# Query features transposed by DMA instead of on TensorE, with the loads planned as one DMA stream, in a linear-attention and feed-forward kernel

One core of a Trainium2 chip. The metric is the device time of one execution in microseconds (us), median of several runs. A run is called slow when it is over 1.5% above the fastest of its kernel in the same session; ratios use the fast runs only.

## The reference

Attention with sketched quadratic features, then a gated feed-forward layer. Cut to what matters:

```python
# q, k, v: (4, 4, 1088, 32); S1, S2: (8, 32); w_gate, w_val: (128, 1536); w_out: (1536, 128)
def phi(x):                                   # 64 features
    a = einsum('rd,bhsd->bhsr', S1, x); b = einsum('rd,bhsd->bhsr', S2, x)
    return einsum('bhsi,bhsj->bhsij', a, b).reshape(*x.shape[:-1], 64)
kv = einsum('bhsf,bhsd->bhfd', phi(k), v);  z = sum(phi(k), axis=2)
attn = (phi(q) @ kv) / (phi(q) . z + 1e-6)
x = attn.transpose(0, 2, 1, 3).reshape(4352, 128)
out = (maximum(x @ w_gate, 0) * (x @ w_val)) @ w_out
```

## The kernel before

The tokens are split into ten *groups* (three of batch 0, two of each later batch, one of remainders). A group needs `kv` of its batch; then its query features `qp` (tokens on partitions) are transposed into `pt` (features on partitions), multiplied by `kv` (`num`), and evacuated into `xT`. The feed-forward part works on `xT` in 102 *units*: gate matmul, relu on ScalarE, value matmul, product `ht` on VectorE, output matmul. The groups start at units 0, 6, 12, 24, 36, 48, 60, 72, 84 and 96.

No engine chooses its order at run time. A planner in the program, `plan()`, sorts all operations by durations written beside them and by `SEM`, the delay it assumes from the end of an operation to its use on another engine. Each engine then works through its fixed list. A gate ties attention work to a unit.

```python
# class Q
def tr(self, x):                     # TensorE: 8 transposes of 128x128 for a group of 4 tiles
    n = self.n
    self.ps = bank(x).bitcast(FP16)[:, 0:2 * n * 128].rearrange("f (k t) -> f k t", t=128)
    for k in range(2 * n):
        nc.tensor.transpose(self.ps[:, k], self.qp[:, 2 * k:2 * k + 2].rearrange("s r f -> s (r f)"), ident)
def tre(self, lo, hi):               # ScalarE: evacuation, twice for a group of 4 tiles
    if lo == 0:
        self.pt = a_kp.tile([128, 2 * self.n, 128], FP16, name="pt")
    nc.scalar.copy(out=self.pt[:, lo:hi], in_=self.ps[:, lo:hi])
# ...
SEM = {"PE": 220.0, "ACT": 220.0, "DVE": 250.0, "POOL": 200.0}
K0, KA, KB, QA, QB = 2, 35, 25, 20, 8
# ... in add_k: half of the first batch's products kp on VectorE
dve = first and hf == 0
phis.append(op("DVE" if dve else "POOL", 640 if dve else 1080, kb.phi, hf, ...))
# ... in add_q
tr = op("PE", 115 * c, qk.tr, deps=tuple(phis), bank=banks, **kw)
tres = [...]                         # op("ACT", 600, qk.tre, ...)
num = op("PE", ..., qk.num, deps=(tre, *kv), bank=banks, **kw)
spread(n0, start[grp] - QA, start[grp] - QB)      # gates of a group's q work
```

## Time and profile before

| | before |
|---|---|
| time | 125.57 us median (124.8 to 126.27), span of the profiled run 123.9 us |
| busy | PE 114.9 us, DVE 97.3, ACT 81.3, POOL 46.8 |
| first feed-forward matmul (gate) | 22.11 us |
| transposes on PE, evacuations on ACT | 68, 17 |

PE is TensorE, DVE VectorE, ACT ScalarE, POOL GpSimd, SP SyncE, which only issues DMA here. A timeline row gives start, duration, engine, line and operation; the bracket at its end is the engine's idle time before it and what ended it. This row of PE's timeline, before, is the end of the start phase:

```profile
22.11 0.38 PE L454 MATMUL bank<-xT,wg 128*128 128x256 f16 x2 [0.48 <-ACT xT L433]
```

### The profile page before, as it was taken

What the parts mean: (1) busy time and instruction counts of PE and PEld (TensorE: products, weight loads), DVE (VectorE), ACT (ScalarE), POOL (GpSimd) and SP (SyncE); (2) the same over time, 40 slices, a digit from 0 to 9 for tenths busy, and PEclk for the clock granted to TensorE, in tenths of its full rate; (3) what the DMA queues carried; (4) which work ended last, traced back from release to release, by engine and by line L of the source; (5) the groups of instructions that cost most, each with busy time, mean ns of one, the idle gap of its engine ahead of it and who ended that gap; (6) DMA issues with size and microseconds to landing.
All of it is one profiled execution on the core that took longest, in us unless ns stands there. A gap on an engine that the chain in (4) does not pass through costs nothing.

```text
span 123.9 us, 2888 instructions
## 1 busy us (share of the span) xinstructions
PE 114.9 (93%) x1117; PEld 80.6 (65%) x1117; DVE 97.3 (78%) x198; ACT 81.3 (66%) x165; POOL 46.8 (38%) x62
## 2 busy tenths in 40 slices
PE   6994899889999999999999999999999999999940
PEld 6864748767877669765665568755655766667920
DVE  3589376587889889397999796788979998979940
ACT  4100004795865649698996578659979988989930
POOL 6959102600593179941510199117005404000000
PEclk9999559999999999999999999999999999999995
DMA  2999990554053507562002100120020011011022
GB/s 49 300 141 192 181 224 6 176 107 158 9 188 55 105 0 177 77 156 100 14 0 41 49 3 0 11 79 0 3 52 33 8 28 57 5 19 65 0 44 83
DMA packets 9521, 9.28 MB, mean 75 GB/s; under 512 B 3364, under 2 KB 7844, under 8 KB 9508
## 3 DMA queue, kind: packets, MB, share of 16 engines
q1 hardware_dynamic: 5228, 6.82, 18.7%
q0 software_dynamic: 4096, 2.25, 14.2%
q8 instruction: 8, 0.13, 0.4%
q10 hardware_dynamic: 184, 0.04, 0.1%
q14 instruction: 5, 0.04, 0.1%
HBM read 9.12 MB, written 2.23 MB: 92 GB/s over the span
## 4 chain that ended last, share of the span: by engine, by line
PE 74%; DVE 11%; DMA 5%; ACT 4%; issue 2%; SPq 1%; ACTq 0%
PE bank L454 16%; PE bank L481 16%; PE bank L466 15%; PE bank L372 8%; DVE ht L471 8%; PE bank L254 5%; DMA q_sb<-in_q_dram 5%; PE bank L409 3%; ACT g_sb L460 2%; PE bank L427 2%; PE bank L302 2%; PE bank L280 2%; PE bank L334 2%; PE bank L155 2%; PE bank L312 1%
## 5 line engine op out<-in xcount | busy, mean ns | idle before, releaser
L471 DVE TENSOR_TENSOR ht<-g_sb,bank 128x512 f16<-128x512 f16 x102 | 65.7, 676 | 11.3 <-ACT g_sb L460 5.3
L460 ACT ACTIVATE g_sb<-bank 128x512 f16<-128x512 f32 x102 | 60.0, 602 | 15.7 <-PE bank L454 13.7
L481 PEld LDWEIGHTS <-ht 128*128 128x128 f16 x408 | 30.3, 98 | 18.4 <-issue 2.0
L481 PE MATMUL bank<-wo,ht 128*128 128x128 f16 x408 | 39.3, 219 | 0.6 <-DVE ht L471 0.6
L454 PE MATMUL bank<-xT,wg 128*128 128x512 f16 (+1 forms) x120 | 38.7, 347 | 0.6 <-ACT xT L433 0.5
L466 PE MATMUL bank<-xT,wv 128*128 128x512 f16 (+1 forms) x120 | 38.3, 347 | 0.4 <-DVE ht L471 0.4
L202 POOL TENSOR_TENSOR qp<-an,abq 128x1024 f16<-128x1024 f32 (+1 forms) x9 | 15.8, 1757 | 8.7 <-DVE an L397 8.1
L202 POOL TENSOR_TENSOR kp<-abk 128x512 f16<-128x512 f32 x14 | 14.5, 1064 | 8.5 <-DVE abk L265 8.5
L384 POOL TENSOR_TENSOR bw<-abq 128x128 f32<-128x128 f32 (+1 forms) x7 | 3.1, 436 | 31.7 <-DVE abq L380 31.7
L466 PEld LDWEIGHTS <-wv 128*128 128x128 f16 x120 | 11.7, 99 | 3.3 <-issue 1.6
L454 PEld LDWEIGHTS <-wg 128*128 128x128 f16 x120 | 11.5, 100 | 3.3 <-issue 2.0
L372 PE MATMUL bank<-qt,wst 128*128 128x512 f32 (+2 forms) x26 | 11.4, 553 | 0.0
L416 ACT COPY pt<-bank 128x512 f16<-128x512 f16 x17 | 10.0, 596 | 1.4 <-PE bank L409 1.4
L254 PE MATMUL bank<-kt,sk 128*128 128x256 f32 x32 | 9.6, 396 | 0.0
L380 DVE STREAM_TRANSPOSE abq<-bank 128x512 f32<-128x512 f32 (+1 forms) x10 | 6.3, 633 | 2.9 <-PE bank L372 2.9
L155 PE MATMUL bank<-zero 128*128 128x128 f16 x88 | 7.5, 256 | 1.1 <-DVE maskw L142 1.1
L155 PEld LDWEIGHTS <-zero 128*128 128x128 f16 x88 | 6.7, 117 | 1.4 <-DVE maskw L142 1.1
L246 DVE STREAM_TRANSPOSE kt<-k_sb 128x512 f32<-128x512 f32 x8 | 5.5, 698 | 1.9 <-DMA k_sb<-in_k_dram 1.9
L324 ACT ACTIVATE kv<-bank 64x64 f16<-64x64 f32 x16 | 3.5, 218 | 5.2 <-PE bank L292 5.0
L433 ACT CAST xT<-bank 128x512 f16<-128x512 f32 (+1 forms) x10 | 5.3, 529 | 2.3 <-PE bank L427 2.2
L280 PEld LDWEIGHTS <-kp 128*128 128x128 f16 x64 | 4.2, 112 | 3.5 <-DVE kp L202 1.9
L280 PE MATMUL bank<-v_sb,kp 128*128 128x64 f16 x64 | 4.8, 206 | 1.8 <-DVE kp L202 1.8
(73 smaller groups left out, 98.7 us busy)
## 6 DMA issues: line engine op xcount, KB each, us to landing
q_sb<-in_q_dram SPq DMA_DIRECT2D x4, 544.0 KB, 7.5
out_dram<-o_sb SPq DMA_DIRECT2D x7, 256.0 KB
k_sb<-in_k_dram SPq DMA_DIRECT2D x3, 512.0 KB, 4.6
v_sb<-in_v_dram POOLq DMA_DIRECT2D x4, 256.0 KB, 5.9
k_sb<-in_k_dram SPq DMA_DIRECT2D x2, 256.0 KB
wg<-in_moe_w_gate_dram POOLq DMA_DIRECT2D x1, 384.0 KB, 7.3
wv<-in_moe_w_val_dram POOLq DMA_DIRECT2D x1, 384.0 KB, 8.6
wo<-in_moe_w_out_dram POOLq DMA_DIRECT2D x1, 384.0 KB, 10.2
```

The costliest lines, as they stand in the source:

```text
L155: nc.tensor.matmul(w_ps[:, 0:128], zero, zero, start=True, stop=True)
L202: eng.tensor_tensor(out=dst.rearrange("s x (i j) -> s x i j", i=R), in0=a_src[:, :, :, None].to_broadcast([dst.shape[0], n, R, R]), in1=ab ...
L254: nc.tensor.matmul(self.ps[h0][:, lo * n * 32:(lo + w) * n * 32].rearrange("p (c x) -> p c x", c=w), sk[:, hf].rearrange("p a b f -> p (a ...
L280: nc.tensor.matmul(self.m[:, p * 64:p * 64 + 64], self.kp[:, hf, c * H + 2 * p:c * H + 2 * p + 2].rearrange("s h f -> s (h f)"), v_sb[self ...
L372: nc.tensor.matmul(self.ps[:, i * w:(i + 1) * w], wst[:, b].rearrange("p h f -> p (h f)"), self.qt.rearrange("p x t -> p (x t)")[:, i * w: ...
L380: nc.vector.transpose(self.absb.rearrange("p x f -> p (x f)"), self.ps[:, 0:n * 128])
L416: nc.scalar.copy(out=self.pt[:, lo:hi], in_=self.ps[:, lo:hi])
L454: nc.tensor.matmul(g_ps[:, y * W:(y + 1) * W], wg[:, j], xT[:, self.col:self.col + W], start=True, stop=True)
L460: nc.scalar.activation(out=self.g_sb, in_=self.g_ps, func=ACTF.Relu)
L466: nc.tensor.matmul(self.v_ps[:, y * W:(y + 1) * W], wv[:, j], xT[:, self.col:self.col + W], start=True, stop=True)
L471: nc.vector.tensor_tensor(out=self.ht, in0=self.g_sb, in1=self.v_ps, op=ALU.mult)
L481: nc.tensor.matmul(o[:, s], self.ht[:, y * W + x * 128:y * W + (x + 1) * 128], wo[:, j], start=(j == 0 and s == 0), stop=(j == NJ - 1), sk ...
```

## The change

The intent: take the query transposes off TensorE, the bound, and their evacuations off ScalarE; let SyncE issue DMA transposes instead. The planner now also sees the loads, as operations of a DMA stream. With it come new distances, another share of work at the start, and another order of the k side. Cut to its core:

```diff
+        def turn(self):
+            self.pt = a_kp.tile([128, 2 * self.n, 128], FP16, name="pt")
+            nc.sync.dma_start(out=self.pt, in_=self.qp.rearrange("s x f -> s (x f)"), transpose=True)
-    SEM = {"PE": 220.0, "ACT": 220.0, "DVE": 250.0, "POOL": 200.0}
+    SEM = {"PE": 220.0, "ACT": 220.0, "DVE": 250.0, "POOL": 200.0, "DMA": 2000.0, "SP": 2000.0}
-    K0, KA, KB, QA, QB = 2, 35, 25, 20, 8
+    K0, KA, KB, QA, QB = 3, 33, 21, 17, 12
+    def load(ns, eng, t, fn, *args, **kw):
+        o = op(eng, t, fn, *args, **kw)
+        return op("DMA", ns, lambda: None, deps=(o,))
     # add_k: first batch's kp all on POOL, half of its kv copies on DVE, z's remainder first
-                dve = first and hf == 0
-                phis.append(op("DVE" if dve else "POOL", 640 if dve else 1080, kb.phi, hf, ...
+                phis.append(op("POOL", 1120 if first else 1080, kb.phi, hf, nc.gpsimd, c, 2, ...
     # add_q
-        tr = op("PE", 115 * c, qk.tr, deps=tuple(phis), bank=banks, **kw)
-        ...
+        if fast:
+            tr = op("PE", 115 * c, qk.tr, deps=tuple(phis), bank=banks, **kw)
+            ...
+        else:
+            tres = [op("SP", 1250, qk.turn, deps=tuple(phis), **kw)]
+            hold("qp", an, tres[0])
+            tre = tres[0]
-                g0 = start[grp] <= 12
+                g0 = start[grp] < 12
     # ... cut: loads wrapped in load(), buffers g 3 and v 3, smaller re-estimates
```

By the words of the change the first three groups stay on TensorE. The last edit makes it two: the group that starts at unit 12 goes by DMA as well, so there are eight DMA transposes.

More of the change, by code (lines that the diff above doesn't have):

```diff
@@ L284, in kv @@
                         v_sb[self.b][:, 2 * p:2 * p + 2, cc * D:(cc + 1) * D],
-                        start=c == 0 and hf == 0 and p == 0, stop=False,
+                        start=c == 0 and hf == 0 and p == 0, stop=c == GC - 1 and hf == 1,
                         skip_group_check=True)
@@ L295, in kv_rest @@
                         vt[rows, 2 * p:2 * p + 2, e * D:(e + 1) * D],
-                        start=False, stop=e == E - 1, skip_group_check=True)
+                        start=False, stop=False, skip_group_check=True)
         def z(self, x, c):
-            if c == 0:
+            if x is not None:
                 self.zps = bank(x)[:, 0:64]
@@ L305, in z, with z_rest @@
                 ab.rearrange("s h (a f) -> s a h f", a=2)[:, :, :, R:2 * R],
-                start=c == 0, stop=False, skip_group_check=True)
-        def z_rest(self, rest):
+                start=x is not None, stop=False, skip_group_check=True)
+        def z_rest(self, x, rest):
+            if x is not None:
+                self.zps = bank(x)[:, 0:64]
             rows = slice(32 * self.b, 32 * self.b + 32)
@@ L313, in z_rest @@
                     self.zps[:, 0:32], ab.rearrange("s h f -> s (h f)"), ab[:, :, R:2 * R],
-                    start=False, stop=e == E - 1, skip_group_check=True)
+                    start=x is not None and e == 0, stop=e == E - 1, skip_group_check=True)
         def zdiag(self):
@@ L320, in zdiag, with kvcopy @@
                 in1=maskz.rearrange("p a h j -> p (a h j)"), op=ALU.mult)
-        def kvcopy(self, g, r):
-            nc.scalar.mul(
-                out=kv16[64 * r:64 * r + 64, self.b, r].rearrange("f (p g) d -> f p g d", g=2)[
-                    :, :, g],
-                in_=self.m[64 * g:64 * g + 64, 0:128].rearrange("f (p g d) -> f p g d", p=2, g=2)[
-                    :, :, g],
-                mul=KVSCALE)
+        def kvcopy(self, g, r, eng):
+            o = kv16[64 * r:64 * r + 64, self.b, r].rearrange("f (p g) d -> f p g d", g=2)[:, :, g]
+            i = self.m[64 * g:64 * g + 64, 0:128].rearrange("f (p g d) -> f p g d", p=2, g=2)[
+                :, :, g]
+            if eng is nc.scalar:
+                eng.mul(out=o, in_=i, mul=KVSCALE)
+            else:
+                eng.tensor_scalar(out=o, in0=i, scalar1=KVSCALE, scalar2=None, op0=ALU.mult)
         def w(self, x):
@@ L411, in tr @@
                     self.qp[:, 2 * k:2 * k + 2].rearrange("s r f -> s (r f)"), ident)
+        def turn(self):
+            self.pt = a_kp.tile([128, 2 * self.n, 128], FP16, name="pt")
+            nc.sync.dma_start(out=self.pt, in_=self.qp.rearrange("s x f -> s (x f)"),
+                              transpose=True)
         def tre(self, lo, hi):
@@ L508, in __init__ @@
             self.holds, self.end = [], None
-    SEM = {"PE": 220.0, "ACT": 220.0, "DVE": 250.0, "POOL": 200.0}
+    SEM = {"PE": 220.0, "ACT": 220.0, "DVE": 250.0, "POOL": 200.0, "DMA": 2000.0, "SP": 2000.0}
     SLACK = (0.0, 60.0, 60.0, 0.0)
-    BUFS = {**dict.fromkeys(range(8), 1), "g": 2, "v": 4, "o": 2, "kt": 3, "qt": 3, "abk": 2, "abq": 2, "kp": 2,
+    BUFS = {**dict.fromkeys(range(8), 1), "g": 3, "v": 3, "o": 2, "kt": 3, "qt": 3, "abk": 2, "abq": 2, "kp": 2,
             "qp": 2, "ktr": 3, "pt": 2, "g_sb": 4, "ht": 8, "bw0": 1, "bw1": 1, "an": 2, "rd": 2, "zd": 2}
@@ L589, with add_rest @@
         units += [F(*grp, i) for i in range(NJ * grp[2] // 4)]
-    T0 = {"PE": 4700.0, "DVE": 2900.0, "ACT": 5300.0, "POOL": 7900.0}
+    T0 = {"DMA": 16500.0, "SP": 4700.0, "PE": 4700.0, "DVE": 2900.0, "ACT": 5300.0, "POOL": 7900.0}
     WGAP, WARM_UNTIL = 250.0, 16000.0
-    K0, KA, KB, QA, QB = 2, 35, 25, 20, 8
-    def add_rest(n, src, at, level, gate):
+    K0, KA, KB, QA, QB = 3, 33, 21, 17, 12
+    def load(ns, eng, t, fn, *args, **kw):
+        o = op(eng, t, fn, *args, **kw)
+        return op("DMA", ns, lambda: None, deps=(o,))
+    def add_rest(n, src, at, level, gate, loaded=()):
         x = Rest(n, src)
         kw = dict(level=level, gate=gate)
-        t1 = op("DVE", 360, x.t1, at=at, **kw)
+        t1 = op("DVE", 360, x.t1, at=at, deps=loaded, **kw)
         ab = op("PE", 240, x.ab, deps=(t1, sk_fill), bank=range(7), **kw)
@@ L604, in add_rest, with add_k @@
         return x, t2, phi
-    def add_k(b, rest, landed, gate, banks, loaded, behind):
+    def add_k(b, rest, landed, gate, banks, k_in, v_in, behind):
         kb = K(b)
@@ L613, in add_k @@
         for pr in range(2):
-            t1s.append(op("DVE", 620, kb.t1, pr, at=landed[pr], deps=tuple(t1s[-1:]), level=lv, **kw))
+            t1s.append(op("DVE", 620, kb.t1, pr, at=landed[pr], deps=(*t1s[-1:], *k_in), level=lv, **kw))
         n = 2 if first else 4
@@ L622, in add_k @@
                                   deps=(*t1s[h0 // 2:(h0 + n) // 2], sk_fill, *abs_[-1:], *behind),
-                                  bank=(None,) if new else banks, level=lv, **kw))
+                                  bank=(None,) if new else banks, level=(3 if h0 == 0 else 2) if first else 0, **kw))
                     abs_.append(new[-1])
@@ L630, in add_k @@
             for hf in range(2):
-                dve = first and hf == 0
-                phis.append(op("DVE" if dve else "POOL", 640 if dve else 1080, kb.phi, hf,
-                               nc.vector if dve else nc.gpsimd, c, 2, deps=tuple(t2s), level=lo_lv, **kw))
+                phis.append(op("POOL", 1120 if first else 1080, kb.phi, hf, nc.gpsimd, c, 2,
+                               deps=tuple(t2s), level=lo_lv, **kw))
         zs = []
+        if first:
+            zs.append(op("PE", 500, kb.z_rest, x, deps=(rest_t2,), level=lv, bank=banks, **kw))
         for c in range(GC):
-            zs.append(op("PE", 330, kb.z, c, deps=(*t2s, *zs[-1:]), level=lv,
+            zs.append(op("PE", 275, kb.z, c, deps=(*t2s, *zs[-1:]), level=lv,
                          bank=(None,) if zs else banks, **kw))
-        zs.append(op("PE", 500, kb.z_rest, x, deps=(zs[-1], rest_t2), level=lv, **kw))
+        if not first:
+            zs.append(op("PE", 500, kb.z_rest, x, deps=(zs[-1], rest_t2), level=lv,
+                         bank=(None,), **kw))
         zd = op("DVE", 200, kb.zdiag, deps=(zs[-1],), level=lv, **kw)
@@ L645, in add_k @@
         for c in range(GC):
-            kvs.append(op("PE", 280, kb.kv, c, bank=(None,) if kvs else banks,
-                          deps=(*phis[c // 2 * 2:c // 2 * 2 + 2], *kvs[-1:], *loaded), level=lo_lv, **kw))
-        kvs.append(op("PE", 300, kb.kv_rest, x, vt, deps=(kvs[-1], rest_phi), level=lo_lv, **kw))
-        hold("abk", t2s[0], kvs[-2])
-        hold("kp", t2s[0], kvs[-2])
+            kvs.append(op("PE", 240, kb.kv, c, bank=(None,) if kvs else banks,
+                          deps=(*phis[c // 2 * 2:c // 2 * 2 + 2], *kvs[-1:], *v_in), level=lv, **kw))
+            if c == 0:
+                kvs.append(op("PE", 300, kb.kv_rest, x, vt, deps=(kvs[-1], rest_phi), level=lo_lv, **kw))
+        hold("abk", t2s[0], kvs[-1])
+        hold("kp", t2s[0], kvs[-1])
         cps = []
@@ L653, in add_k, with add_q @@
             for r in range(2):
-                cps.append(op("ACT", 210, kb.kvcopy, g, r, deps=(kvs[-1], *cps[-1:]), level=lo_lv, **kw))
+                dve = first and g == 1
+                cps.append(op("DVE" if dve else "ACT", 230, kb.kvcopy, g, r,
+                              nc.vector if dve else nc.scalar, deps=(kvs[-1],), level=lv, **kw))
         hold("bank", kvs[0], cps[-1])
+        for c in cps[:-1]:
+            cps[-1].deps += (c,)
         return cps[-1], wf
-    def add_q(grp, n, kv, wf, landed, gate, fast, banks):
+    def add_q(grp, n, kv, wf, landed, gate, fast, banks, q_in):
         qk = Q(*grp, n)
@@ L663, in add_q @@
         rest = grp[0] == B
-        t1 = op("DVE", 560 if rest else 40 + 145 * c, qk.t1, at=landed, **kw)
-        ab = op("PE", 1000 if rest else 60 + 110 * c, qk.ab, deps=(t1, *wf), bank=banks, **kw)
+        t1 = op("DVE", 560 if rest else 40 + 145 * c, qk.t1, at=landed, deps=q_in, **kw)
+        ab = op("PE", 1000 if rest else 60 + 215 * c, qk.ab, deps=(t1, *wf), bank=banks, **kw)
         hold("qt", t1, ab)
@@ L680, in add_q @@
         hold("an", an, phis[-1])
-        tr = op("PE", 115 * c, qk.tr, deps=tuple(phis), bank=banks, **kw)
-        hold("qp", an, tr)
-        tres = []
-        for lo in range(0, 2 * c, 4):
-            tres.append(op("ACT", 600, qk.tre, lo, lo + 4, deps=(tr, *tres[-1:]), **kw))
-        tre = tres[-1]
-        hold("bank", tr, tre)
+        if fast:
+            tr = op("PE", 115 * c, qk.tr, deps=tuple(phis), bank=banks, **kw)
+            hold("qp", an, tr)
+            tres = []
+            for lo in range(0, 2 * c, 4):
+                tres.append(op("ACT", 600, qk.tre, lo, lo + 4, deps=(tr, *tres[-1:]), **kw))
+            tre = tres[-1]
+            hold("bank", tr, tre)
+        else:
+            tres = [op("SP", 1250, qk.turn, deps=tuple(phis), **kw)]
+            hold("qp", an, tres[0])
+            tre = tres[0]
         num = op("PE", 1000 if rest else 50 + 65 * c, qk.num, deps=(tre, *kv), bank=banks, **kw)
@@ L735, in load_rest_q, with load_rest_kv @@
         load_q(nc.sync, b)
-        if b == 1:
-            load_rest(nc.sync, kr, k, range(B))
-            load_rest(nc.sync, vr32, v, range(B))
+    def load_rest_kv():
+        load_rest(nc.sync, kr, k, range(B))
+        load_rest(nc.sync, vr32, v, range(B))
     sketch = Sketch()
@@ L748 @@
     f0 = op("DVE", 420, fill_static, deps=(s_copy,), level=1)
-    rest0 = (*add_rest(32, kr0, 6000.0, 2, -1), vr0)
-    rest = (*add_rest(128, kr, 26000.0, 0, 7), vr)
-    cast = op("ACT", 400, lambda: nc.scalar.copy(out=vr, in_=vr32), gate=9, at=29000.0)
-    kvs, wfs, xs = [], [], []
+    rest0 = (*add_rest(32, kr0, 5500.0, 2, -1), vr0)
+    cast = None
+    kvs, wfs, xs, qs = [], [], [], []
     for b in range(B):
         s = start[b, 0, 2 if b == 0 else GC]
-        lv = ()
+        k_in = v_in = q_in = ()
         if b > 0:
-            lv = (op("POOL", 900, load_main, nc.gpsimd, v_sb[b], v, b, gate=[0, -1, 10, 20][b],
-                     at=13000.0), cast)
-            op("ACT", 200, load_k, b, at=13500.0, gate=[0, -1, 4, 20][b])
-            op("ACT", 200, load_rest_q, b, gate=[0, 0, 10, 24][b])
+            k_in = (load(1650, "ACT", 200, load_k, b, at=13500.0, gate=[0, -1, 4, 20][b]),)
+            q_in = (load(1800, "ACT", 200, load_rest_q, b, gate=[0, 0, 10, 24][b]),)
+            v_in = (load(1650, "POOL", 900, load_main, nc.gpsimd, v_sb[b], v, b,
+                         gate=[0, 0, 10, 20][b], at=13000.0),)
+        if b == 1:
+            kvr = load(600, "SP", 3000, load_rest_kv, gate=0)
+            rest = add_rest(128, kr, 0.0, 0, 7, (kvr,))
+            cast = op("ACT", 400, lambda: nc.scalar.copy(out=vr, in_=vr32), gate=9, deps=(kvr,))
+            rest = (*rest, vr)
+        if b > 0:
+            v_in += (cast,)
+        qs.append(q_in)
         n0 = len(ops)
-        kv, wf = add_k(b, rest if b else rest0, [(4300.0, 5300.0), (19500.0,) * 2, (0.0,) * 2, (0.0,) * 2][b],
-                       s - 40 if b > 1 else -1, range(7), lv,
+        kv, wf = add_k(b, rest if b else rest0, (4400.0, 5600.0) if b == 0 else (0.0, 0.0),
+                       s - 40 if b > 1 else -1, range(7), k_in, v_in,
                        (first_ab,) if b == 1 else ())
@@ L774 @@
                               2 if start[grp] == 0 else 1 if g0 else 0,
-                              range(7))
+                              range(7), q_in)
                 xs.append(x)
@@ L782 @@
     x, _ = add_q(groups[-1], len(xs), tuple(kvs), tuple(wfs), 0.0, start[groups[-1]] - 20, 0,
-                 range(7))
+                 range(7), sum(qs, ()))
     xs.append(x)
```

## The prediction

> **What bounds the kernel now.** I read the page first (its slices, then its chain), then the rows of the groups, then the timeline of PE and of VectorE at the start and at the end. The slices:
>
> ```profile
> PE   6994899889999999999999999999999999999940
> POOL 6959102600593179941510199117005404000000
> PEclk9999559999999999999999999999999999999995
> ```
>
> A slice is 3.1 us. From slice 8 (some 25 us) to slice 37 PE never falls below 90%. Before that stands a start of 22 us in which little of the feed-forward part runs, and in two of its slices PE has half its clock. The chain and the rows that matter:
>
> ```profile
> PE 74%; DVE 11%; DMA 5%; ACT 4%; issue 2%; SPq 1%; ACTq 0%
> ...
> L471 DVE TENSOR_TENSOR ht<-g_sb,bank 128x512 f16<-128x512 f16 x102 | 65.7, 676 | 11.3 <-ACT g_sb L460 5.3
> ...
> L202 POOL TENSOR_TENSOR qp<-an,abq 128x1024 f16<-128x1024 f32 (+1 forms) x9 | 15.8, 1757 | 8.7 <-DVE an L397 8.1
> ...
> L416 ACT COPY pt<-bank 128x512 f16<-128x512 f16 x17 | 10.0, 596 | 1.4 <-PE bank L409 1.4
> ```
>
> Three quarters of the chain are PE. A busy PE could still be an idle one whose matmuls are drawn long (379 ns for 512 columns), so I take the distance from start to start instead. At the end of the PE timeline it is 0.22 us for 512 columns and 0.22 us for four of 128, that is 56 ns each; in the chain in order of time eight transposes take 0.45 us, the same 56 ns; an fp32 product of 256 columns takes 0.46 us, one of 512 takes 0.87. With such distances, all matmuls after the first gate matmul (at 22.1 us) come to 94.1 us: 67 for the feed-forward part, 27 for the attention. The last matmul ends at 119.7 us, so this part takes 97.6 us and PE is really at work for 96% of it. PE's throughput bounds it; ScalarE and VectorE do not, though VectorE is near: 83.2 us busy from 22 to 120 us. In the last 10 us a unit costs PE three times 0.22 us and VectorE 0.64 to 0.68 us: a tie.
>
> The start is another thing, a chain of latencies:
>
> ```profile
> 9.92 3.17 DVE L202 TENSOR_TENSOR kp<-abk 128x512 f16<-128x512 f32 x2
> 13.01 0.21 DVE L318 TENSOR_TENSOR zd<-bank,maskz 128x64 f32<-128x64 f32 x1
> 14.38 0.19 DVE L339 TENSOR_TENSOR wst<-bank,maskw 128x32 f32<-128x32 f32 x1 [1.16 <-PE bank L334]
> 15.88 0.45 DVE L380 STREAM_TRANSPOSE abq<-bank 128x256 f32<-128x256 f32 x1 [1.31 <-PE bank L372]
> ...
> 17.38 0.69 DVE L202 TENSOR_TENSOR qp<-an,abq 128x512 f16<-128x512 f32 x1
> ```
>
> Two products kp on VectorE take 3.17 us, and zd, which the q side needs, stands behind them until 13.01 us. It could have run from about 10.6 us on.
>
> **What the Trainium skill says.** "VectorE: DVE Perf Modes", The three transpose paths: a 128x128 transpose of 2-byte data takes 390 ns on TensorE and 1309 ns through the DMA crossbar. The trace agrees on a TensorE latency of that size (L409 is drawn at about 390 ns for a group of four), but pipelined it costs PE only 56 ns; no run yet shows the crossbar. "DMA: Bandwidth & Descriptors", Latency and other measured facts: a DMA transpose was measured at 261 GB/s; and Anatomy of one DMA gives a fixed cost of some 2.0 us (for the GpSimd path). One group's pt is 128x1024 fp16, 256 KB, so my estimate from that page is 1.0 + 2.0 us, and with the sequencer some 3.3 us from issue to landing. The same page, Queues, rings and completion order: an engine takes a ring's descriptors in order. So a transpose on SyncE stands behind the loads that SyncE issued before it; a k load of 512 KB took 4.6 us to land here. "Advanced Engine Details and Errata", GPSIMD Details: GpSimd shares ports with VectorE and conflicts with its instructions of two SBUF inputs. The trace agrees: the 128x512 product took 1.6 us on VectorE beside GpSimd products, and 0.69 us (qp above) with GpSimd idle.
>
> **The change part by part.** The order of instructions shows that the text of the change is off by one: the third group (start at unit 12) also goes by DMA. There are 8 DMA transposes, seven of 128x8x128 and one of 128x4x128; 8 of the 68 PE transposes stay.
>
> 1. *PE.* 60 transposes leave, all from after the first gate: 60 x 56 ns = 3.36 us. Nothing else on PE changes in number but 14 warming matmuls at the start. Work after the first gate is 94.1 - 3.3 = 90.8 us; at the same 96%, 94.2 us in place of 97.6: 3.4 us less.
> 2. *ScalarE.* 15 of 17 evacuations leave: 15 x 596 ns = 8.9 us of 81.3. ScalarE is off the path; worth nothing by itself.
> 3. *VectorE.* Two kp products (3.2 us) go to GpSimd, two kv copies (some 0.45 us) come. All before the first gate, so VectorE's load in the long part stays at 83 us, below PE's 91.
> 4. *The start.* In the new order zd follows the q transposes directly. I step through with the old durations: abk ends at 9.1 us (held by the q load, which lands at 7.97), the two q transposes end at 10.1, zd at 10.6, the w product at 11.5, wst at 11.8, first q product 12.6, abq 13.3, then bw, dn, rd, an and qp as before 2 us more: 15.2 us in place of 18.07. On the other side GpSimd now does kpr and four kp in a row from 8.95 us: five times 1.04 us ends at 14.2, the kv products at 14.8, the copies, shared by two engines, at about 16.2. So PE transpose 15.5, evacuation to 16.5, num at 17.0, xT at 17.5: first gate at about 17.8 us, or later if the clock falls to half as before. I put 18.2 in place of 22.1: 3.9 us less. This, not the transposes, is the larger half.
> 5. *What it adds.* On the latency of a group: before, tr, evacuation twice and the semaphores took some 2.2 us; now 0.2 + 3.3 us. Where a group's num stands close behind its qp in PE's fixed order, PE waits. Two places look tight. Third group: GpSimd's qp ends near 23.9 us by the same stepping, its transpose lands at 27.4, and PE comes to its num after 8.4 us of work, at 27.0: 0.5 us. First group of batch 1 (gate 24): from the q product to the end of qp the trace before shows 4.75 us (41.75 to 46.49); plus 3.5 us is 8.3, and the new order gives PE 7.4 us of work between: 0.7 us. The groups after have about 10 us or more of work between. With loads in the ring before them I give 1.7 us in all.
>
> Sum: 125.57 - 3.9 - 3.4 + 1.7 = 120.0 us.
>
> **The rivals.** *First: the transpose is slow, and its wait takes the place of the one removed.* If one takes 6 us or more, alone or behind a k or q load, each group waits some 2 to 3 us at least in the two tight places and about 1 us in some of the other six: 5 to 9 us, and 123 to 127 us in all. For it: no trace shows one, and SyncE is one in-order queue with loads and stores, each with its own wait on ScalarE; before, its stores wait for ScalarE for up to 13 us. Against it: DMA is busy only 0 to 2 tenths after slice 22, and the order lets most groups have their features many units early. *Second: VectorE becomes the bound.* PE's saving comes in stretches where attention is dense; in the others the two tie at 0.65 us a unit, and PE's saving turns into waits for ht. For it: the tail's tie, and VectorE at 7.7 of 8 us from 94 to 102 us. Against: from 46 to 54 us VectorE has 5.7 of 8. This would halve the 3.4: 121.7 us. *Third: the start gains little*, as PE falls to half its clock again and GpSimd's four kp set the pace; first gate at 20.5 us, 122.3 us in all. Before, two slices at half clock follow a gap of 1.76 us on PE; the new order has warming matmuls in its gaps, which speaks against. *Fourth, to the good side*: no tight place waits, 118.3 us, and a first gate at 17 us makes 117.
>
> **Range and chances.** The terms' errors are about 1.2 us for the start, 1 for PE's share, and 2 to the bad side for the transposes. I take 117.0 to 123.5 us. Faster by over 2% means below 123.06 us; it needs about 2.5 of the 7.3 us of gains to survive, and only a slow transpose with a failed start undoes it: 0.87. Within 2% 0.09, slower 0.04.
>
> **What would show each step.** Right: first gate matmul at 17 to 19 us; zd at about 10.5 us; PE idle near 27 us and ahead of the num at gate 24, each at most 1.5 us; transposes landing in 3 to 4.5 us; VectorE's busy time lower by about 2.5 us and ScalarE's by about 9; last matmul near 114 us. Wrong: waits of PE for pt from the DMA of more than 3 us in sum (first rival), more idle of PE for ht in the middle at a prompt pt (second), half clock from 12 to 18 us and a first gate past 20 us (third).

## The result

| | before | changed |
|---|---|---|
| median, runs side by side | 125.92 us (4 runs, 124.8 to 127.82) | 129.74 us (129.28 to 129.88, and a slow run of 135.12) |
| ratio | 1 | 1.032, 95% interval 1.022 to 1.043: slower |
| first gate matmul | 22.11 us | 17.33 us |
| last output matmul starts | 119.3 us | 122.5 us |
| busy | PE 114.9, DVE 97.3, ACT 81.3, POOL 46.8 | PE 111.3, DVE 95.2, ACT 74.3, POOL 49.7 |

A ratio is the mean time of one kernel's fast runs over the mean of the other's of the same rounds, so it isn't quite the ratio of the medians. The output is correct.

The page of the changed kernel: PE and its clock in 40 slices (3.2 us each), the engines of the chain that ended last, and the row of `num`:

```profile
PE   6999689935999999699999769993999999999940
PEclk9999999995599999769999999999999999999995
PE 50%; DMA 18%; DVE 11%; POOL 11%; issue 4%; ACT 2%; DVEq 1%; SPq 0%; POOLq 0%
L437 PE MATMUL bank<-pt,kv 128*32 128x256 f16 (+2 forms) x104 | 4.0, 249 | 7.6 <-DMA pt<-qp 7.6
```

Against the lines of before: the solid row of 9s has holes; PE's part of the chain fell from 74% to 50%, and DMA transposes took 18%. PE stood 7.6 us ahead of `num`, all of it waiting for `pt`. Who waited for whom (total, times, longest), first PE's longest wait of before from 24 us to 104 us, then that of the changed kernel:

```profile
PE bank L466 <- DVE ht L471: 0.4, 1, 0.4
```

```profile
PE bank L437 <- DMA pt<-qp: 7.6, 4, 3.5
```

The start went as planned. The changed kernel's timeline:

```profile
9.56 4.13 POOL L202 TENSOR_TENSOR kp<-abk 128x512 f16<-128x512 f32 x4
...
10.34 0.23 DVE L321 TENSOR_TENSOR zd<-bank,maskz 128x64 f32<-128x64 f32 x1 [0.58 <-PE bank L303]
...
14.57 0.69 DVE L202 TENSOR_TENSOR qp<-an,abq 128x512 f16<-128x512 f32 x1
...
17.33 0.38 PE L464 MATMUL bank<-xT,wg 128*128 128x256 f16 x2 [0.48 <-ACT xT L443]
```

`zd` runs at 10.34 in place of 13.01 us, and the feed-forward part begins 4.8 us earlier. So the changed kernel needs 127.5 - 17.3 = 110.2 us from there to its end, before 123.9 - 22.1 = 101.8 us: 8.4 us more for the same feed-forward work and 3.4 us less of transposes. The chain in order of time shows where (start, length; the pieces of DMA alone):

```profile
22.86 7.13 DMA pt<-qp
...
47.96 3.65 DMA pt<-qp
...
67.81 6.51 DMA pt<-qp
...
82.99 5.44 DMA pt<-qp
```

Each is the time from a transpose's issue to its landing, the moment at which the engine that waits is told that the data are there. What happens around the first, in windows (stretch, length; busy time of PE, PEld, DVE, ACT, POOL; clock; DMA share; GB/s):

```profile
27.00:30.00 3.00, 0.00 (x0) 0.00 (x0) 0.73 (x2) 0.00 (x0) 2.75 (x3) 0.80 1.26 215
30.00:33.00 3.00, 2.97 (x20) 2.00 (x21) 1.56 (x3) 0.58 (x1) 1.78 (x3) 0.50 0.36 138
33.00:36.00 3.00, 3.00 (x18) 2.31 (x18) 0.95 (x2) 0.60 (x1) 0.68 (x1) 0.56 0.00 0
```

PE does nothing for 3 us, and then works at half clock for nearly 6 us more. The Trainium skill, "TensorE: Matmul & The Clock Gate", Part 1: The HAM clock gate, says that about 3.4 us without activity gate the clock to half, and that it needs a busy window of that size to come back. This trace agrees in kind: a gap of 3.51 us, then 0.50 and 0.56. It doesn't agree on the threshold. The mean of 0.80 from 27 to 30 us is 0.6 us of lost clock, so 1.2 us at half: the clock fell at about 28.8 us, only 2.3 us into the gap that began at 26.5. At 52.7 us it fell after gaps of 0.39 and 0.68 us, and after those of 1.76 and 1.99 us (at 74.37 and 88.56 us) it stayed at 1.00. What decides isn't shown here.

### The profile page after: what moved, and what is told of

It reads as the page before. It is cut to its first block, busy times and chain, and to the rows that moved or that the text cites. A ratio compares the mean times of both kernels' runs of the same rounds, so it can differ in the third digit from the quotient of the medians.

```text
span 127.5 us, 2813 instructions
## 1 busy us (share of the span) xinstructions
PE 111.3 (87%) x1043; PEld 76.8 (60%) x1043; DVE 95.2 (75%) x196; ACT 74.3 (58%) x148; POOL 49.7 (39%) x66
## 3 DMA queue, kind: packets, MB, share of 16 engines
HBM read 9.12 MB, written 2.23 MB: 89 GB/s over the span
## 4 chain that ended last, share of the span: by engine, by line
PE 50%; DMA 18%; DVE 11%; POOL 11%; issue 4%; ACT 2%; DVEq 1%; SPq 0%; POOLq 0%
DMA pt<-qp 18%; PE bank L476 11%; PE bank L491 10%; PE bank L464 10%; DVE ht L481 6%; POOL qp L202 5%; PE bank L155 4%; PE bank L376 3%; POOL kp L202 3%; PE bank L437 2%; PE bank L254 2%; PE bank L303 2%; DVE abq L384 1%; PE bank L338 1%; POOL v_sb L87 1%
## 5 line engine op out<-in xcount | busy, mean ns | idle before, releaser
L470 ACT ACTIVATE g_sb<-bank 128x512 f16<-128x512 f32 x102 | 59.2, 598 | 21.9 <-PE bank L464 17.7
L491 PEld LDWEIGHTS <-ht 128*128 128x128 f16 x408 | 31.2, 100 | 18.5 <-issue 1.4
L476 PE MATMUL bank<-xT,wv 128*128 128x512 f16 (+1 forms) x120 | 40.0, 358 | 0.1
L202 POOL TENSOR_TENSOR kp<-abk 128x512 f16<-128x512 f32 x16 | 16.5, 1061 | 6.4 <-DVE abk L265 6.4
L464 PEld LDWEIGHTS <-wg 128*128 128x128 f16 x120 | 12.3, 103 | 3.0 <-issue 1.5
L437 PE MATMUL bank<-pt,kv 128*32 128x256 f16 (+2 forms) x104 | 4.0, 249 | 7.6 <-DMA pt<-qp 7.6
L376 PE MATMUL bank<-qt,wst 128*128 128x512 f32 (+2 forms) x26 | 9.6, 471 | 0.0
L437 PEld LDWEIGHTS <-kv 128*32 128x32 f16 x104 | 1.5, 95 | 11.5 <-DMA pt<-qp 7.0
L499 ACT ACTIVATE o_sb<-bank 128x512 f32<-128x512 f32 (+1 forms) x10 | 5.3, 532 | 3.8 <-PE bank L491 3.8
L401 POOL TENSOR_TENSOR an<-abq,rd 128x128 f32<-128x128 f32 (+1 forms) x8 | 3.1, 390 | 9.2 <-DVE rd L396 9.2
```

The lines of the kernel that those rows point to most:

```text
L202: eng.tensor_tensor(out=dst.rearrange("s x (i j) -> s x i j", i=R), in0=a_src[:, :, :, None].to_broadcast([dst.shape[0], n, R, R]), in1=ab ...
L376: nc.tensor.matmul(self.ps[:, i * w:(i + 1) * w], wst[:, b].rearrange("p h f -> p (h f)"), self.qt.rearrange("p x t -> p (x t)")[:, i * w: ...
L437: nc.tensor.matmul(o[32 * h:32 * h + 32, i * w:(i + 1) * w], kv16[:, b, r, h], self.pt[:, i * w:(i + 1) * w, 32 * h:32 * h + 32], start=Tr ...
L464: nc.tensor.matmul(g_ps[:, y * W:(y + 1) * W], wg[:, j], xT[:, self.col:self.col + W], start=True, stop=True)
L470: nc.scalar.activation(out=self.g_sb, in_=self.g_ps, func=ACTF.Relu)
L476: nc.tensor.matmul(self.v_ps[:, y * W:(y + 1) * W], wv[:, j], xT[:, self.col:self.col + W], start=True, stop=True)
```

## The experiments

The question after the result: is it the plan, the traffic of the transposes, or their lateness; and why are they late, when the one at 93.1 us landed in 2.8 us?

First four. Before on that chip: 125.32 us median of 7.

**e1, no DMA transposes, new plan.**

```diff
-        if fast:
+        if True:
```

> The changed kernel with every group's features turned on PE again (no DMA transpose at all); the new plan stays. Theory A (the transposes land late, because they stand in SyncE's one ring behind loads and stores, and PE's fixed order waits for them and then runs at half clock) and theory B (a DMA transpose is slow by itself or slows its neighbours): the waits for pt go, the early first gate (17.3 us) stays, PE does 3.3 us more: about 121 us. Theory C (the new plan's order is the loss, whoever turns the features): 126 us or more.

Measured: 120.43 us (119.97 to 120.81), ratio 0.963 (0.956 to 0.971). First gate at 17.54 us, no wait for `pt`, clock 0.995. The plan alone gains 4.9 us, all of it in the start: from the first gate to the end e1 takes 119.1 - 17.5 = 101.6 us, as long as before. The DMA transposes, with the order that the planner makes around them, cost the changed kernel 9.2 us. Theory C falls.

**e2, the third group on TensorE too.**

```diff
-        if fast:
+        if fast or start.get(grp) == 12:
```

> The changed kernel with the third group too turned on PE, as the words of the change say. Theory A: the wait of 3.5 us near 30 us and the half clock after it go, at the price of 0.45 us of PE; the later waits (0.4, 1.8, 2.0 us) stay: 124 to 126 us. Theory B: the same here. Theory C: 129 us, and the gap near 30 us stays for another cause.

Measured: 135.32 to 135.60 us in the fast runs, and 143.12 for the profiled one, whose start was slow (see e11). A miss for every theory: the wait near 30 us went, yet the time grew by 6 us. The planner had shuffled everything after it, and the other transposes met worse places: PE waited four times for `pt`, 12.1 us in all. **e12** is the same text once more, for a profile without the slow start:

> e2 once more, the same text, for a profile with the first gate at 17.5 us, which e2's profiled run lacked. Theory A2: transposes issued within 1 us of a store's issue land after 6 to 6.5 us; PE waits some 10 us for pt in all, more than the changed kernel's 7.6, because the new order leaves less work ahead of each num; 135 us.

Measured: 142.64 us, with the slow start again (first gate at 23.36 us), so that aim was missed; but the same four waits, 11.8 us in all, stand in it. Of its stores and transposes on SyncE's queue two pairs are typical: store issued at 70.41, transpose at 71.17, `num` released at 77.52 us; store at 86.58, `num` at 93.66 us.

**e3, the loads and stores off SyncE's ring.**

```diff
-        load_main(nc.sync, k_sb[b], k, b)
+        load_main(nc.scalar, k_sb[b], k, b)
     # likewise load_q of the later batches, and the stores of the main groups
```

> The changed kernel with the later k and q loads and the big stores issued from ScalarE, so that after the start SyncE's ring carries the transposes and the small kr and vr loads only. Theory A: each transpose lands in 2.8 to 4 us (in place of up to 7.1), PE's waits for pt fall from 7.6 to below 2 us: 121 to 124 us. Theory B (transposes slow by themselves, or by sharing the 16 DMA engines whatever the ring): landing times stay at 5 to 7 us beside a load or store, and the time at 128 us or more. ScalarE pays some 16 issues of 0.4 to 0.6 us.

Measured: 129.14 and 130.82 us in the fast runs (134.3 and 145.2 in slow ones). Theory A in its first form falls: the order within one ring is not the cause. PE still waited 8.0 us, and a transpose on SyncE's ring was late beside a store on ScalarE's. From its two rows, the issue of the store (ScalarE's queue) and PE's `num` after it; the transpose was issued at 68.11 us and landed after 6.6 us:

```profile
67.97 0.55 ACTq L502 DMA_DIRECT2D out_dram<-o_sb  x1
```

```profile
74.80 0.40 PE L437 MATMUL bank<-pt,kv 128*32 128x256 f16 x8 [0.49 <-DMA pt<-qp]
```

The skill's "DMA: Bandwidth & Descriptors", Queues, rings and completion order, says two things that matter here: an engine takes turns between the rings that have work, and the write that reports a DMA's completion lands only after every earlier write of that engine, across its queues. In the prediction I had leaned on ring order alone. The second rule would let a store on any ring delay the report of a transpose. The 6.6 us here don't need it: the packets (at the end of the experiments) show that the data themselves came late.

**e4, DMA transposes alone, in the plan of before.**

```diff
+        if start.get(grp) not in (0, 6, 12):
+            tres = [op("SP", 1250, qk.turn, deps=tuple(phis), **kw)]     # and turn(), SEM["SP"] = 2000
```

> The kernel before with only the DMA transposes in place of PE's for the groups after the third (SyncE 1.25 us and 2.0 us to landing in its plan). Theory A: PE has 2.9 us less work, but some transposes stand behind a store and come 2 to 4 us late: 124 to 128 us. Theory B: 127 us or more, with every transpose late. Theory C (plan, not transposes): 122.5 us.

Measured: 127.37 us (126.86 to 127.54), ratio 1.018 (1.011 to 1.026), by the 2% rule unclear, by the interval slower. 2.9 us less work for PE turned into 2 us more. One wait of 2.0 us stands out, ahead of the first group of batch 1, whose transpose (issued at 46.08 us, right after a k load at 45.38) landed after 5.7 us; a stretch at half clock follows (mean 0.51 from 52.7 to 56.2 us). In the profiles, e4 takes 124.8 - 21.6 = 103.2 us from the first gate to the end, where 101.8 - 2.9 = 98.9 would be before's time without these transposes. Of the 4.3 us between, the wait and the lost clock (3.5 x 0.49 = 1.7 us) make some 3.7 by this estimate.

So a second form of theory A: **A2, a transpose alone lands in under 3 us, but one issued beside another large transfer, on whatever ring, lands when that one is done; the plan allows 3.25 us.** Next four; before on that chip 125.72 us.

**e5, stores cut to 16 KB**.

```diff
-                        "(k s) t m -> k t s m", s=n),
-                    in_=o_sb[:, 0:n])
+                        "(k s) t m -> k t s m", s=n)[0, :, 0:1],
+                    in_=o_sb[0:32, 0:1])
```

> The changed kernel with its stores of the main groups cut to 16 KB each (wrong result on purpose; same instructions in the same order). Theory A2 (a transpose lands late when another large transfer is in flight, on whatever ring, since alone it lands in 2.4 to 2.8 us): the two transposes issued at 67.8 and 83.0 us, which landed after 6.5 and 5.4 us with a 256 KB store in flight, land in under 3.5 us; PE's waits for pt fall from 7.6 to about 4 us; the wait near 30 us, beside loads, stays: 125 to 127 us. Rival (lateness has nothing to do with the stores): no change in landing, 129.5 us.

Measured: 123.16 and 124.69 us in fast runs (two slow ones at 126.89 and 128.4), 5.0 to 6.6 us less than the changed kernel and less than either theory said. The view of the tile `pt` and PE's waits:

```profile
DMA to landing us min/median/max: 2.4/2.8/3.5
```

```profile
PE bank L437 <- DMA pt<-qp: 4.9, 2, 4.6
```

The order of instructions is the same, only the stores are small: the two late transposes beside stores are now in time (the landing line covers those whose landing the trace shows). The first one, beside loads, still costs 4.6 us. This shows that stores made the later ones late. The clock from 52 to 58 us, 0.62 and 0.81 in the changed kernel (below), is 1.00 here.

**e6, the traffic without the wait**: e1, plus the same eight DMA transposes into a tile that nobody reads.

```diff
+            if self.col >= 4 * 128:
+                unread = a_kp.tile([128, 2 * n, 128], FP16, name="unread")
+                nc.sync.dma_start(out=unread, in_=self.qp.rearrange("s x f -> s (x f)"), transpose=True)
```

> The variant with all features turned on PE (e1, 120.4 us) plus the same eight DMA transposes of the same tiles, issued at the same places, into a tile that nobody reads; every engine but SyncE keeps its order. Theory A2 (what costs is PE waiting for a late pt, not the traffic): 120 to 121.5 us, same as e1. Theory B (the transposes' traffic itself slows loads, stores or the engines): 123 us or more.

Measured: 120.29 and 120.67 us in its fast runs (two slow ones at 126.6 and 126.8), e1's time. The traffic costs nothing. Theory B falls; what costs is the waiting.

**e7, only where there is time, and with time allowed.**

```diff
-        if fast:
+        if fast or start.get(grp) <= 36:
-    ... "SP": 2000.0}
+    ... "SP": 4500.0}
-    K0, KA, KB, QA, QB = 3, 33, 21, 17, 12
+    K0, KA, KB, QA, QB = 3, 33, 21, 22, 14
```

> The changed kernel with the groups up to the one that starts at unit 36 turned on PE, only the later five (48, 60, 72, 84, 96) by DMA, the plan told 4.5 us to landing after the issue in place of 2.0, and the q work of a group begun earlier (22 to 14 units ahead in place of 17 to 12). Theory A2: a pt planned for 5.75 us after its features is in time nearly always, PE's waits for pt below 1 us, and 36 transposes (2.0 us of PE) less than e1: 117.5 to 119.5 us. Theory B: no better than e1 with the same gates, 121 us or more.

Measured: 118.18 and 118.49 us in fast runs (two slow ones at 124.6 and 125.0). No wait of PE for `pt` at all. In these fast runs it is faster than both kernels.

**e8, the control for e7's distances**: e1 with `QA, QB = 22, 14`.

> e1 (all turned on PE) with the q work begun 22 to 14 units ahead in place of 17 to 12: the control for e7's gates. Both theories: within 1 us of e1, 119.5 to 121 us; if it is as fast as e7, the gates and not the transposes gained there.

Measured: 126.09 to 126.50 us, all four. A miss: all four had the slow start (first gate at 23.44 us in its profile), so it decided nothing. But it gave the slow start away. PE's first rows, e8 and then e7 in a fast run:

```profile
1.06 3.81 PE L155 MATMUL bank<-zero 128*128 128x128 f16 x34 [1.06 <-DVE maskw L142]
...
6.25 2.02 PE L254 MATMUL bank<-kt,sk 128*128 128x256 f32 x4
```

```profile
1.06 3.50 PE L155 MATMUL bank<-zero 128*128 128x128 f16 x34 [1.06 <-DVE maskw L142]
...
5.65 1.13 PE L254 MATMUL bank<-kt,sk 128*128 128x256 f32 x4 [0.17 <-DVE sk L181]
```

The same four fp32 matmuls take 2.02 us in e8 and 1.13 in e7: PE works at half its clock. (The first row alone doesn't tell: e1 and the changed kernel also have 3.81 us there, and their fp32 matmuls run at full clock.) It goes on until about 20 us, and the first gate comes at 23.44 us instead of 16.91, 6.5 us later. The clock row of the page doesn't show it; this is e8's:

```profile
PEclk9999999999999999999999999999999999999996
```

So the *slow start*: the 34 warming matmuls at the head of the program (on zeros, read by nobody) sometimes fail to bring PE to full clock. The profiles of e2, e6, e8 and e12 show it directly, all in plans with the new start. Where a slow run of such a kernel wasn't profiled (the changed kernel's 135.12 us, for one, 5.5 us over its others), I infer it from the 6 us. From the first gate to the end e8 takes 124.8 - 23.4 = 101.4 us and e7 116.5 - 16.9 = 99.6, so these distances by themselves gain nothing over e1 (101.6), and the five DMA transposes of e7 gain 1.8 us, by one profile of each.

Four more. Before on that chip: 125.33 us median of 11.

**e9, the changed kernel with the later loads moved away from the first transpose.**

```diff
-            k_in = (load(..., load_k, b, at=13500.0, gate=[0, -1, 4, 20][b]),)
+            k_in = (load(..., load_k, b, at=13500.0, gate=[0, -1, 13, 20][b]),)
     # likewise the q loads (10 to 13) and the v loads (10 to 13) of batch 2
```

> The changed kernel with the loads of batch 2 (k, q, v) begun at unit 13 in place of units 4 and 10, so that the first DMA transpose (issued near 22.9 us) goes out before them. Theory A2: it lands in some 3 to 4 us in place of 7.1, PE's wait of 3.5 us near 30 us and the half clock after it shrink to under 1 us; the later waits beside stores remain (4 us, with some shift): 123 to 126 us. Rival (the first transpose is late for another cause): the wait near 30 us stays over 3 us, 129 us.

Measured: 131.26 to 131.78 us in fast runs (one slow, 139.29). The mechanism came as expected, the time didn't. PE's two rows of `num` after the first transpose (issued at 22.61 us) and after its worst one:

```profile
27.19 0.40 PE L437 MATMUL bank<-pt,kv 128*32 128x256 f16 x8 [0.47 <-DMA pt<-qp]
...
107.02 0.40 PE L437 MATMUL bank<-pt,kv 128*32 128x256 f16 x8 [3.42 <-DMA pt<-qp]
```

The wait that was 3.51 us is 0.47: loads had made the first transpose late. But the plan moved again: three waits beside stores are 2.23, 2.41 and 3.42 us, and one of 1.74 us follows a transpose issued 3.4 us after a q load.

**e10, e7's choice of groups without its time**: `"SP": 2000.0` and `QA, QB = 17, 12` again, all else as e7.

> e7 (only the five late groups by DMA, 118.2 and 118.5 us in its fast runs) with the plan's 2.0 us to landing and the changed kernel's own distances (17 to 12 units). Theory A2: the late groups' transposes beside a 256 KB store land after 5 to 6.5 us again, planned for 3.25: PE waits 2 to 5 us in all for pt, 120 to 123 us in fast runs. Rival (the choice of groups alone made e7 fast, not the time allowed): 118.3 us and no waits.

Measured: 128.30 us in one run, 131.2, 132.63 and 138.34 in the others; the first gate of the profiled one (132.63) stands at 17.46 us, so the start wasn't slow. Every run is longer than the 120 to 123 us that theory A2 said, and why the four differ so much isn't shown. PE's waits for `pt`, in the profiled run:

```profile
PE bank L437 <- DMA pt<-qp: 9.1, 3, 4.6
```

With the same five transposes, e7 waits for none. So the choice of groups didn't make e7 fast, but the times at which its plan issues and uses the transposes (4.5 us allowed in place of 2, gates 14 to 22 units ahead in place of 12 to 17). Two things changed there at once, which these runs don't part: `num` comes later after its transpose, and no 256 KB transpose stands close behind a store any more (the nearest follows 4.9 us after one; the last, half as large, follows after 2.2 us and lands after 4.1; here three follow after 0.6 to 1.0 us, and one took 7.7 us to land).

**e11, e7 with a longer warm-up.**

```diff
-    WARM0 = 34
+    WARM0 = 56
```

> e7 with 56 warming matmuls at the start in place of 34. Theory W (the slow runs of the new plan, 6 us longer, are those in which the 3.8 us of warming matmuls did not bring PE to full clock, so that PE ran at half clock from 5 to 20 us): with some 1.2 to 2 us more of them all runs start at full clock, no run near 124.8 us, fast runs 0.5 to 1 us longer than e7's: 118.5 to 119.5 us. Rival (the slow runs come from elsewhere): slow runs in some of the six still.

Measured: 119.14 to 120.24 us in all six runs, ratio 0.971 (0.961 to 0.982; by the 2% rule unclear, as one run of before was 122.6 us and only it and those near it counted as fast). No slow start, no wait for `pt`; the first gate is at 18.93 us, 2 us later than in e7. That is more than was said: the median of 120.18 us is 1.8 us over e7's fast runs, not 0.5 to 1.

Two things were open after these twelve: what the transposes are worth when nothing waits (e8 hadn't told by time), and whether a shorter warm-up holds. Two last ones; before on that chip 125.58 us median of 7.

**e13, e8 with 56 warming matmuls**, the control of e11.

> e8 (all features turned on PE, q work begun 22 to 14 units ahead) with 56 warming matmuls, so that the start is the same as e11's. Theory A2 with the prediction's term for PE (a transpose costs PE 56 ns, 36 of them 2.0 us): 2 us longer than e11, 121.5 to 122.5 us. Rival (the gain of e7 over e1 is the gates): 120.2 us, as e11.

Measured: 120.51 to 122.05 us, median 121.37, ratio 0.967 (0.960 to 0.975), no slow start. From the first gate to the end it takes 120.2 - 19.0 = 101.2 us, e11 118.5 - 18.9 = 99.6. So by one profile each, both pairs (e8 and e7, e13 and e11) say 1.6 to 1.8 us for 36 transposes moved off TensorE and waited for by nobody. The profiled run of e13 is its longest; by the medians of all runs e13 takes 1.2 us more than e11, just under what theory A2 said. So the worth is 1.2 to 1.8 us; counted at 56 ns each, 2.0.

**e14, e7 with 44 warming matmuls.**

> e7 with 44 warming matmuls, between its 34 (half of the runs start at half clock) and e11's 56 (none of six). Theory W: fewer slow starts than with 34, perhaps still one of four; fast runs 118.4 to 119.5 us, between e7's and e11's.

Measured: 118.69 to 120.20 us, median 118.86, ratio 0.951 (0.942 to 0.960). First gate at 17.46 us, no slow start, no wait for `pt`. The view of the tile `pt`, five transposes, none of 256 KB close behind a store:

```profile
DMA to landing us min/median/max: 2.8/3.4/4.1
```

This is the best version here: the new start, transposes by DMA for the five late groups, issued early enough. With 34 warming matmuls (e6, e7, e8) 8 of 12 runs were some 6 us longer; with 44 or 56 (e11, e13, e14) none of 14 was. That is a count, not a proof that 44 always suffice, and the twelve ran on another chip than the fourteen. On the chip of the fourteen, with 34, e12's one run had the slow start and one of e9's four was 7.6 us longer; on a third chip e1 had none in four. And e13's profile shows a late rise of the clock:

```profile
1.06 6.08 PE L155 MATMUL bank<-zero 128*128 128x128 f16 x56 [1.06 <-DVE maskw L142]
...
7.89 1.08 PE L254 MATMUL bank<-kt,sk 128*128 128x256 f32 x4
```

All 56 took 109 ns each, half rate (e8's 34 took 112; at full clock it is 56 ns), and the fp32 matmuls after them run at full clock. In e11 (5.96 us for 56) it came little earlier. By my estimate a warm-up of 44 would have ended at about 5.9 us (1.06 + 44 x 0.109), before that rise.

**What a neighbour does to a transpose**, from the rows of all these runs (256 KB each, as the stores are):

| case | us from the transpose's issue to landing or to `num` |
|---|---|
| nothing beside it: changed at 93.1 us, e4 | 2.8, 2.7 |
| small stores (e5) | 2.4 to 3.5 |
| store issued 0.75 and 1.7 us before, same ring: changed | 6.5, 5.4 |
| store issued 0.1 us before, another ring: e3 | 6.6 |
| store issued 2.2 us before, 128 KB transpose: e7, e14 | 4.1, 4.1 |
| beside loads: changed (first), e4, e3 | 7.1, 5.7, 8.9 |

With a store ahead, `num` is released 7.0 to 7.3 us after the *store's* issue: changed 67.06 to 74.37 and 81.27 to 88.56, e9 61.63 to 68.87 and 77.93 to 85.24, e10 61.84 to 68.86 and 76.26 to 83.60, e12 70.41 to 77.52 and 86.58 to 93.66. (In e10 and e12 one more each took 8.5 and 8.6 us.) So the transpose lands when the store is done. It isn't a lack of bandwidth, as the windows of the changed kernel around the transpose of 67.81 us show (columns as above):

```profile
68.00:71.00 3.00, 3.00 (x24) 2.04 (x22) 3.00 (x6) 2.04 (x5) 0.00 (x0) 1.00 0.24 40
71.00:74.00 3.00, 1.61 (x6) 0.52 (x4) 2.05 (x4) 0.85 (x2) 0.45 (x1) 1.00 0.91 135
```

For 3 us the DMA engines are a quarter busy at 40 GB/s, 0.12 MB; most of the two transfers' 0.52 MB moves only after that. Is it the data that are late, or only the report that they have landed? The packets tell: the transpose's are under 512 B, the store's 2 KB. From the view `--dma` of the changed kernel, 67.0 to 70.4, 70.4 to 72.9 and 72.9 to 75.0 us:

```profile
DMA packets 29, 0.06 MB, mean 17 GB/s; under 512 B 0, under 2 KB 0, under 8 KB 29
...
DMA packets 563, 0.32 MB, mean 128 GB/s; under 512 B 464, under 2 KB 464, under 8 KB 563
...
DMA packets 596, 0.14 MB, mean 69 GB/s; under 512 B 596, under 2 KB 596, under 8 KB 596
```

For 2.6 us after its issue no packet of the transpose moves, and more than half move after the store's last. The one at 93.13 us, alone, moved from 94.3 to 95.4. e3, with the store on another ring, shows the same: no small packet before 70.6 us, 621 after 73.3. So beside a store the data are late, not only the report. The store is slow by itself: before, with no transpose near, the one issued at 64.22 us moved until 69.5. In e4, beside loads, it is otherwise: 1040 small packets moved from 48.6 to 50.1 us, 48 after, and `num` was released only at 51.87; there the report was late, which the skill's rule on completions (under e3) would allow. Why a store holds up a transpose's data, on whatever ring, stays open.

## Why the prediction was wrong

- **Step 4, the start: right.** First gate 17.33 us where 18.2 was said, 4.8 us gained where 3.9 was; `zd` at 10.34 where 10.5 was said. e1 shows it alone: 4.9 us faster.
- **Step 1, TensorE: right in count, too large.** 1.2 to 1.8 us of the counted 2.0 for 36 transposes; scaled to 60, 2.0 to 3.0 us in place of 3.4 (an estimate).
- **Steps 2 and 3: right that neither engine is on the path.** ScalarE 7.0 us less busy where 8.9 was said, VectorE 2.1 where 2.5 was.
- **Step 5, what the change adds: this failed.** It said "I give 1.7 us in all". The third group's transpose was to land at 27.4 us and landed at 30.0, after 7.1 us: a wait of 3.51 us in place of 0.5. The rest of that line was near (issue at 22.86 us, PE ready at 26.5 where 27.0 was said); the 3.3 us to landing failed. Gate 24 was right (0.39 and 0.68 us where 0.7 was said). "The groups after have about 10 us or more of work between" was plainly wrong: PE reached the `num` of the transposes issued at 67.8 and 83.0 us so early that it waited 1.76 and 1.99 us. The duration of a lone transpose was estimated well (2.8 us for 3.0 to 3.3); I put it in for transposes that have a store or load beside them, where it is 5.4 to 7.1.
- **A term not in the sum at all: the clock after a wait.** PE works on at 0.50 and 0.56 after the first wait and, at the stretch of gate 24, where it also has gaps, at 0.62 and 0.81:

```profile
52.00:55.00 3.00, 2.32 (x15) 1.43 (x11) 1.31 (x4) 1.86 (x4) 2.22 (x4) 0.62 0.45 97
55.00:58.00 3.00, 3.00 (x30) 1.87 (x30) 1.98 (x4) 1.59 (x3) 0.57 (x1) 0.81 0.96 160
```

Lost in these four windows of 3 us: 3 x (0.50 + 0.44 + 0.38 + 0.19) = 4.5 us. My estimate of the balance: 7.6 us of waits + 4.5 of clock - 2.0 to 3.0 of transposes saved = 9.1 to 10.1 us; the changed kernel minus e1 is 129.6 - 120.4 = 9.2 us, though in two sessions. So close a fit is partly luck: in the stretch at 52 us PE was busy for only 2.32 of 3 us, so not all of the clock lost there was wanted.

- **The rivals.** The first had the mechanism (a slow transpose behind other transfers, its wait in place of the work removed) and said 5 to 9 us of waits (measured 7.6) and 123 to 127 us; without the clock the time was still too short, and its ring order isn't the cause (e3). I gave it too little weight, because the DMA engines were nearly idle; idle engines said nothing about latency. The second, VectorE as the bound, isn't seen: e14 gains by the transposes. The third, a failing start, is wrong for the fast runs and right for those with a slow start, by another cause than the one I gave: the 34 warming matmuls don't always suffice.
- **Two readings in the prediction were off, without weight for the sum.** PE's row shows an 8 in slice 8, so its 90% hold from slice 9 (28 us) on. And the 390 ns of L409 are the span of four transposes; one is drawn at 219 ns, so the trace does not agree with the page's 390 for one.
- **Open:** why a store holds up a transpose's data; what sets the clock after a short gap; and which of e7's two changes (the later `num`, or the distance to the stores) does the work.

## What to carry to other kernels

A DMA's duration by itself isn't its latency beside other transfers: allow, in a fixed plan, for the load or store that will be in flight, or issue it where nothing waits soon. Work taken off the bound is worth its time only as long as nothing waits for its replacement; a stall of TensorE can cost clock as well (3 x (0.50 + 0.44) = 2.8 us after the one of 3.51 us, nothing seen after those of 1.76 and 1.99). Look at the rows of the first matmuls after the warm-up, not only at the clock row, to see whether it has worked.

## What the Trainium skill lacked or had wrong

- "DMA: Bandwidth & Descriptors" gives a rate for a DMA transpose but no latency beside other transfers. A 256 KB transpose alone took 2.4 to 2.8 us, a little under the 3.0 us estimated from the page's rate and fixed cost; behind a 256 KB store 5.4 to 6.6 us, beside loads 5.7 to 8.9 us. The page does say that DMAs from several engines run on the same DMA engines and interleave; e3 (6.6 us on a ring of its own) agrees.
- No page gives the time of a single store to HBM: before, one of 256 KB, issued at 64.22 us, moved until 69.5; a 256 KB transpose issued 0.75 us after a 256 KB store landed 3.7 us later than alone, while for 3 us the DMA share was 0.24.
- "TensorE: Matmul & The Clock Gate" says that about 3.4 us of activity bring full clock, that the count varies from run to run, and for a benchmark it advises a warm-up of at least 4 us. Here 3.4 to 3.8 us of warming matmuls (34) weren't enough in 8 of 12 runs, and half clock then lasted to about 20 us; 4.4 us (44) were enough in 4 of 4, but in e13 full clock came only after some 6 us. The page's gap of about 3.4 us isn't what decides here: the clock fell 2.3 us into a gap, and at 52.7 us after gaps of 0.39 and 0.68.
- The same page warns that clock events in a trace are not to be fully trusted. e8 is a case: its clock row shows full clock while fp32 matmuls take twice their time (2.02 for 1.13 us).
- "VectorE: DVE Perf Modes" gives 390 ns for one 128x128 transpose on TensorE; before, one is drawn at 219 ns (L409). It also gives a time for one by DMA; no run here has a single one.
